# Converting float64 weights with bit operations on VectorE, and moving GpSimd's sums and low parts to VectorE

## The chip, the cores and the metric

The kernel runs on one core of a Trainium2 chip. Five engines work beside each other: TensorE (matmuls into PSUM), VectorE and ScalarE (elementwise work), GpSimd (elementwise work, on SBUF only) and SyncE, which here issues all DMAs. The metric is the device time of one execution in microseconds (us); less is better.

## The reference

Two stages of layers over q, k and v of shape (2, 6016, 256) in float32. The weights are float64 arrays.

```python
qn = q / (np.linalg.norm(q, axis=1, keepdims=True) + 1e-06)
kn = k / (np.linalg.norm(k, axis=1, keepdims=True) + 1e-06)
s = kn.transpose(0, 2, 1) @ qn / tau          # 256 x 256 for each batch
a = softmax(s)                                # rows, with 1e-9 in the divisor
x = (v @ a).reshape(12032, 256)
h = x @ w_in                                  # w_in 256 x 2048
x = (h - np.tanh(h)) @ w_out                  # w_out 2048 x 256
gate = 1 / (1 + np.exp(-(x @ w_gate)))        # w_gate, w_val 256 x 1536
out = (gate * (x @ w_val)) @ w_out2           # w_out2 1536 x 256
```

## The kernel before

**Tiling.** The tokens are cut into 24 blocks of 512 (12 for each batch). For a block, `emit_H` makes h for one of 16 column tiles of w_in, `emit_E` h - tanh(h) (two ScalarE squares L309 and L312, a tanh L310, a mask L313, and four VectorE instructions L314 to L317), `emit_gs` splits the result into two float32r parts (high: rounded by ScalarE, L322; low: the difference, L323), `emit_X` multiplies by w_out. `emit_GV` multiplies the block's result by one of 12 column tiles of w_gate and w_val, `emit_S` applies the sigmoid and the product (L387, L388), `emit_ps` splits it, `emit_O` multiplies by w_out2. Each of these products is made of three float32r matmuls of parts: high x high, low x high, high x low. v is split as a block (`split_v`), and so is the result of w_out (`emit_x2`). For block 0, and for the first two column tiles of its last product, the low parts are made by GpSimd, for all others by VectorE.

**The start.** Batch 0's q and k come in 19 chunks of mostly three tiles of 128 tokens, through six buffers (L498). TensorE adds up k^T q (`boot_s`, L507). ScalarE squares each chunk (L515) into one of two buffers, and the squares are added up in accb (L519): q's half by GpSimd, k's by VectorE, in the chunks 0 to 13; both by VectorE in 14 to 17. The last sums are joined (L521, L523), and `norm_mm` sums them over the partitions (L184). TensorE's queue has these matmuls ahead of the last chunk's products. The softmax (`s_softmax`) follows, and then a @ w_in, made once for each batch in chunks (`aw_chunk`), whose low part (L266) H needs.

**Weights.** `conv` brings a piece of float64 weights as pairs of 32-bit words. From the high word come sign, exponent and 20 bits of the mantissa: its absolute value (ScalarE, L121), a clamp (L124), mask and shift (L125), the sign (L128), all as bits of a float32. From the low word: ScalarE makes it a float (L122), VectorE takes the exponent of the first part (L131), GpSimd multiplies the two (L132); that is what the first part lacks. For w_in's eight pieces VectorE adds both (L135). For the 26 pieces of the other weights ScalarE rounds the first part to float32r (L137), and GpSimd makes the low part with a subtraction and an addition (L138, L139).

**Order.** The schedule is written by hand; every engine executes its instructions in the order of the program. A loop over steps T runs through the column tiles of all blocks: in a step stand H of tile T, E of tile T - 1, the split and X of tile T - 2, and pieces of the second layer of the block before. `conv` is a generator whose stages are spread over the steps through `at(step, ...)` and the list `running`: the DMA in one step, the first part in the next, the rounding and low parts in the one after. w_out's pieces are converted in the steps -1 to 13, w_in's last two in steps 6 and 8, those of the second layer from step 15 to 32, one for each step. Four of w_in's pieces are converted between the chunks of the start and two within the softmax. `e_mm` puts products of batch 1's first tokens into steps in which TensorE would wait. The tile pool cv has four buffers, of which a conversion takes two (bt and pt). Batch 1's squares are summed by GpSimd (L602), in the later blocks.

Of the kernel before, what the change touches and what calls it, by code (L numbers as in the profile page):

```python
# [8 lines left out]
F32 = mybir.dt.float32  # L9
F32R = mybir.dt.float32r  # L10
BF16 = mybir.dt.bfloat16
U32 = mybir.dt.uint32
# [5 lines left out]
P = 128  # L18
# h - tanh(h) = h^3 (C2 ((h^2 + CB)^2 + CG)) to 5e-7 for |h| <= HT; beyond HT the difference itself.
HT = 0.25  # L20
# [6 lines left out]
def kernel(  # L27
# [13 lines left out]
    nc = tc.nc  # L41
# [53 lines left out]
    def warm(n, name):  # L95
        """Matmuls that only keep the PE's clock up while it would wait."""
        o = psw(name, (P, P))
        for _ in range(n):
            MM(o, ones, ones, start=True, stop=True)

    aw_hi = [wp.tile([P, NK, 2 * P], F32R, name=f"awh{i}") for i in range(N1 // 2)]
    # until batch 0's a @ w_in is there, its low part's place holds w_in
    win = [wp.tile([P, NK, 2 * P], F32, tag=f"awl{i}", name=f"win{i}") for i in range(N1 // 2)]
# [5 lines left out]
    def conv(src, shape, pool, tag, name, w=None, hi=None, lo=None):  # L109
        """float64 words to float32 (w), or to its two float32r parts (hi, lo): three stages."""  # L110
        a, m = shape
        st = pool.tile([P, a, 2 * m], U32, tag=tag, name=f"st_{name}")
        nc.sync.dma_start(out=st, in_=src)
        yield
        words = st.rearrange("p a (m t) -> p a m t", t=2)
        low, high = words[:, :, :, 0], words[:, :, :, 1]
        bt = cv(f"cb_{name}", (P, a, m))
        pt = cv(f"cp_{name}", (P, a, m))
        bu, pu = bt.bitcast(U32), pt.bitcast(U32)
        lf = low.bitcast(F32)  # L120
        nc.scalar.activation(bt, high.bitcast(F32), AF.Abs)  # L121
        nc.scalar.activation(lf, low, AF.Copy, scale=2.0**-52)  # L122
        yield 1
        nc.vector.tensor_scalar(bt, bt, 2.0**-15, 122879.9921875, ALU.max, ALU.min)  # L124
        nc.vector.tensor_scalar(  # L125
            bu, bu, 0x07FFFFFF, 3, ALU.bitwise_and, ALU.logical_shift_left
        )
        nc.vector.scalar_tensor_tensor(  # L128
            out=bu, in0=high, scalar=0xC0000000, in1=bu, op0=ALU.bitwise_and, op1=ALU.bitwise_or
        )  # L130
        nc.vector.tensor_scalar(pu, bu, 0xFF800000, None, ALU.bitwise_and)  # L131
        nc.gpsimd.tensor_tensor(out=pt, in0=lf, in1=pt, op=ALU.mult)  # L132
        yield
        if w is not None:
            nc.vector.tensor_tensor(out=w, in0=bt, in1=pt, op=ALU.add)  # L135
        else:
            nc.scalar.activation(hi, bt, AF.Copy)  # L137
            nc.gpsimd.tensor_tensor(out=bt, in0=bt, in1=hi.bitcast(F32), op=ALU.subtract)  # L138
            nc.gpsimd.tensor_tensor(out=lo, in0=bt, in1=pt, op=ALU.add)  # L139

    def whole(g):
        """Only the stages of conv."""
        for x in g:
            if x is None:
                yield
# [14 lines left out]

# [1 line left out]
    kq = {}  # L162
# [5 lines left out]
    def s_mm(b, hi, lo, first, last):  # L168
        """hi, lo: [P, 2 (q, k), C] of one tile of tokens."""
        for ct in range(2):  # L170
            cs = slice(ct * P, (ct + 1) * P)
            o = kq[b][:, ct, :]
            MM(o, hi[:, 1, cs], hi[:, 0, :], start=first and ct == 0, stop=False, skip_group_check=True)
            MM(o, hi[:, 1, cs], lo[:, 0, :], start=False, stop=False, skip_group_check=True)
            MM(o, lo[:, 1, cs], hi[:, 0, :], start=False, stop=last, skip_group_check=True)
# [3 lines left out]
    def norm_mm(b, sq, sk, first, last):  # L179
        """Column sums of the tiles of sq (of q's squares) and sk (of k's), on c's partition."""  # L180
        for o, xs in ((0, sq), (2, sk)):
            for i, x in enumerate(xs):
                for ct in range(2):
                    MM(nrm[b][:, o + ct, :], x[:, ct * P:(ct + 1) * P], ones[:, :NW],  # L184
                       start=first and o + i + ct == 0, stop=last and i == len(xs) - 1, skip_group_check=True)

    def s_softmax(b, sq, sk):
        """sq, sk: tiles whose column sums are the sums of squares of q and k."""
        np_ = nrm.get(b)
# [9 lines left out]
        nc.vector.tensor_scalar(rn[:, 2:4], rn[:, 2:4], rtau[:, 0:1], None, ALU.mult)  # L199
        # q's factors as rows, the same on every partition: by the ones' product with their diagonal matrix  # L200
        dg = (cv if b else wk)(f"dg{b}", (P, 2, P))
# [51 lines left out]
    def aw_chunk(b, i, w):  # L253
        """Rows c of a @ w_in, columns of chunk i."""
        ap_ = psw(f"aw{b}_{i}", (P, 2, 2 * P))
        parts = [(aT[b], w)] if b == 0 else [(aT[b][0], w[0]), (aT[b][1], w[0]), (aT[b][0], w[1])]
        for n, (x, y) in enumerate(parts):
            for ct in range(2):
                for kk in range(2):
                    MM(ap_[:, ct, :], x[:, kk, ct * P:(ct + 1) * P], y[:, kk, :],  # L260
                       start=n + ct + kk == 0, stop=n == len(parts) - 1 and kk == 1, skip_group_check=True)
        yield
        if b == 0:
            aw_lo[i] = wp.tile([P, NK, 2 * P], F32R, tag=f"awl{i}", name=f"awl{i}")
        nc.scalar.activation(aw_hi[i], ap_, AF.Copy)
        nc.vector.tensor_tensor(out=aw_lo[i], in0=ap_, in1=aw_hi[i].bitcast(F32), op=ALU.subtract)  # L266

# [1 line left out]
    vn = {}  # L269
# [49 lines left out]

    def split(x, n, name, eng=None):  # L320
        hi, lo = rr(f"{name}h")[:, :n], rr(f"{name}l")[:, :n]
        nc.scalar.activation(hi, x, AF.Copy)  # L322
        (eng or nc.vector).tensor_tensor(out=lo, in0=x, in1=hi.bitcast(F32), op=ALU.subtract)  # L323
        return hi, lo

    def emit_gs(p, f):
        eng = nc.gpsimd if p == 0 else None
        ghl[p, f] = split(g_t.pop((p, f)), blocks[p][2], f"g{p}_{f}", eng)

# [18 lines left out]
    def emit_x2(p):  # L348
# [6 lines left out]
        else:  # L355
            # block 1's come before the last use of block 0's: these are where aT, acc and s1_split's are at other times
            h = [one_p.tile([P, TB], F32R, tag=t, name=f"x2{t}") for t in ("aT", "acc")]
# [33 lines left out]
    def emit_ps(p, m):  # L391
        phl[p, m] = split(p_t.pop((p, m)), blocks[p][2], f"p{p}_{m}", nc.gpsimd if p == 0 and m < 2 else None)

# [29 lines left out]

    # Batch 1's first J0 tiles of tokens, where the PE would wait: native float32 products of
    # what is loaded; their squares are summed later.
    JA, J0, GS = 20, 32, 5
# [37 lines left out]

# [1 line left out]
    rtau = const.tile([P, 1], F32, name="rtau")  # L466
# [12 lines left out]
    with tc.tile_pool(name="boot1", bufs=1) as boot1, tc.tile_pool(name="boot4", bufs=4) as boot4, \  # L479
# [30 lines left out]
        def boot_squares(i):  # L510
            """Squares, summed in accb; the last chunk's are left to the matmuls."""
            j, n = chunks[i]
# [3 lines left out]
            if i == NCH - 1:  # L516
                return [[sq[:, x, jj] for jj in range(n)] for x in range(2)]
            for x, e in enumerate((nc.gpsimd if i < NCH - 5 else nc.vector, nc.vector)):
                e.tensor_tensor(out=accb[:, x, :n], in0=accb[:, x, :n], in1=sq[:, x, :n], op=ALU.add)  # L519
            if i == F2:  # L520
# [7 lines left out]
        def load(i):  # L528
            """Chunk i of q and k, and what of w_in is converted along with it."""
            if i < NCH:  # L530
# [24 lines left out]
        while live:  # L555
            live = [g for g in live if next(g, live) is None]
        # the softmax's stages, and in between what does not wait for them: two of w_in's
        # conversions, v's first parts, batch 1's first products
        sm0 = s_softmax(0, *sq)
# [23 lines left out]

# [1 line left out]
    sraw = {}  # L585
# [44 lines left out]
    def s1_sum():  # L630
        """The sum over a group of tiles to that over all."""
        nc.vector.tensor_tensor(out=ks[1], in0=ks[1], in1=kq[1], op=ALU.add)

# [1 line left out]
    bg = {}  # L635
# [3 lines left out]

    # GV0: the steps of block 0's column tiles of w_gate and w_val; OFF..: those of the others', from  # L640
    # the first step of the block after
    GV0 = (20, 21, 22, 24, 25, 27, 28, 30, 31, 33, 34, 35)
# [140 lines left out]
```

## Time and profile before

| | us |
|---|---|
| median of 3 runs | 2437.92 (2436.18 to 2437.99) |
| the profiled execution: span | 2436.4 |
| TensorE (PE) busy | 2372.4 (97%) |
| VectorE (DVE) busy | 1841.3 (76%) |
| ScalarE (ACT) busy | 1606.9 (66%) |
| GpSimd (POOL) busy | 259.6 (11%) |

The profile gives the profiled execution's own time as its span, from the first instruction to the last; it lies within the three runs. In the rows, PE is TensorE's matmuls and PEld its weight loads. A float32 matmul (not float32r) appears as two instructions. "L314" is line 314 of the kernel. PEclk is the granted TensorE clock as a share of its full 2.4 GHz.

### The profile page before, as it was taken

The numbers are of one execution on the slowest core, as the hardware profiler recorded it, in microseconds if no ns is written. First come the engines' busy times: TensorE is split into PE (matmuls) and PEld (weight loads), VectorE is DVE, ScalarE is ACT, GpSimd is POOL, SyncE is SP. The second block draws the span as 40 slices with busy tenths as digits, with TensorE's granted clock in tenths as the row PEclk, the third lists the DMA queues.
The fourth block names the chain that finished last, engine by engine and source line by source line (L and its number), as shares of the span: only waits on it lengthen the run. The fifth ranks groups of instructions, "written<-read, shape, count | busy, mean of one in ns | idle before, by whom it ended". The sixth has DMA issues, their size and how long they took to land.

```text
span 2436.4 us, 29276 instructions
## 1 busy us (share of the span) xinstructions
PE 2372.4 (97%) x10408; PEld 1935.4 (79%) x10408; DVE 1841.3 (76%) x2791; ACT 1606.9 (66%) x2820; POOL 259.6 (11%) x171
## 2 busy tenths in 40 slices
PE   7868899999999999999999999999999999999999
PEld 6656678878888888788888888888888888888888
DVE  7899977778777777777777777777777777777764
ACT  4766666676766676776666766666666666666663
POOL 6466600111100000000000000000000000000000
PEclk9899999999999999999999999999999999999999
DMA  7432210111110110000100000000000000000000
GB/s 280 139 117 96 74 35 22 39 35 31 52 35 5 44 35 5 18 10 10 44 5 18 16 1 18 18 1 18 18 1 18 18 1 18 18 1 16 1 9 16
DMA packets 49106, 82.62 MB, mean 34 GB/s; under 512 B 4416, under 2 KB 18496, under 8 KB 48960
## 3 DMA queue, kind: packets, MB, share of 16 engines
q1 hardware_dynamic: 48960, 80.76, 10.0%
q8 instruction: 81, 1.33, 0.2%
q14 instruction: 65, 0.53, 0.1%
HBM read 65.80 MB, written 14.94 MB: 33 GB/s over the span
## 4 chain that ended last, share of the span: by engine, by line
PE 87%; DVE 7%; issue 3%; ACT 2%; POOL 1%; DMA 0%; SPq 0%; DVEq 0%; POOLq 0%; ACTq 0%
PE h L298 7%; PE x L344 7%; PE h L301 7%; PE h L299 7%; PE x L342 6%; PE x L341 6%; PE o L406 5%; PE o L405 5%; PE ga L377 5%; PE o L408 5%; PE ga L376 5%; PE va L377 5%; PE va L376 5%; PE va L379 5%; PE ga L379 5%
## 5 line engine op out<-in xcount | busy, mean ns | idle before, releaser
L314 DVE SCALAR_TENSOR_TENSOR w<-u,h 128x512 f32<-128x512 f32 (+1 forms) x384 | 259.1, 675 | 345.5 <-ACT t L310 345.1
L309 ACT ACTIVATE u<-h 128x512 f32<-128x512 f32 (+1 forms) x384 | 223.4, 582 | 256.7 <-PE h L301 256.4
L317 DVE COPY_PREDICATED w<-m,t 128x512 f32<-128x512 uint16 (+1 forms) x384 | 318.3, 829 | 41.0 <-DVE w L316 1.8
L298 PE MATMUL h<-vTh,awh 128*128 128x512 f32 (+1 forms) x768 | 303.8, 396 | 2.7 <-DVE t L315 1.9
L299 PE MATMUL h<-vTh,awl 128*128 128x512 f32 (+1 forms) x768 | 301.0, 392 | 4.2 <-DVE awl L266 4.2
L312 ACT ACTIVATE s<-u,cb 128x512 f32<-128x512 f32 (+1 forms) x384 | 274.0, 713 | 0.0
L313 ACT ACTIVATE m<-u,ct 128x512 bf16<-128x512 f32 (+1 forms) x384 | 272.3, 709 | 0.0
L316 DVE SCALAR_TENSOR_TENSOR w<-s,w 128x512 f32<-128x512 f32 (+1 forms) x384 | 264.3, 688 | 0.0
L315 DVE TENSOR_TENSOR t<-h,t 128x512 f32<-128x512 f32 (+1 forms) x384 | 258.0, 672 | 0.0
L301 PE MATMUL h<-vTl,awh 128*128 128x512 f32 (+1 forms) x768 | 237.6, 391 | 0.0
L310 ACT ACTIVATE t<-h 128x512 f32<-128x512 f32 (+1 forms) x384 | 223.7, 582 | 3.5 <-DVE w L314 0.8
L377 PE MATMUL va<-x2h,wvl 128*128 128x512 f32 (+1 forms) x552 | 216.2, 392 | 0.0
L377 PE MATMUL ga<-x2h,wgl 128*128 128x512 f32 (+1 forms) x552 | 216.1, 392 | 0.0
L376 PE MATMUL ga<-x2h,wgh 128*128 128x512 f32 (+1 forms) x552 | 215.9, 391 | 0.1
L376 PE MATMUL va<-x2h,wvh 128*128 128x512 f32 (+1 forms) x552 | 215.8, 391 | 0.0
L388 DVE TENSOR_TENSOR sg<-va,sg 128x512 f32<-128x512 f32 (+1 forms) x288 | 191.9, 666 | 19.7 <-PE va L379 18.8
L387 ACT ACTIVATE sg<-ga 128x512 f32<-128x512 f32 (+1 forms) x288 | 168.8, 586 | 16.6 <-PE ga L379 12.5
L379 PE MATMUL va<-x2l,wvh 128*128 128x512 f32 (+1 forms) x576 | 178.5, 391 | 0.0
L379 PE MATMUL ga<-x2l,wgh 128*128 128x512 f32 (+1 forms) x576 | 178.0, 390 | 0.0
L298 PEld LDWEIGHTS h<-vTh,awh 128*128 128x128 f32 x768 | 145.2, 189 | 36.6 <-DVE t L315 4.4
L299 PEld LDWEIGHTS h<-vTh,awl 128*128 128x128 f32 x768 | 144.9, 189 | 35.9 <-DVE awl L266 7.5
L301 PEld LDWEIGHTS h<-vTl,awh 128*128 128x128 f32 x768 | 144.2, 188 | 33.3
(396 smaller groups left out, 4772.0 us busy)
## 6 DMA issues: line engine op xcount, KB each, us to landing
v<-in_v_dram SPq DMA_DIRECT2D x22, 512.0 KB, 4.2
out_dram<-ob SPq DMA_DIRECT2D x22, 512.0 KB, 3.0
sr<-in_q_dram SPq DMA_DIRECT2D x47, 128.0 KB, 2.3
sr<-in_k_dram SPq DMA_DIRECT2D x47, 128.0 KB, 2.6
raw<-in_q_dram SPq DMA_DIRECT2D x13, 384.0 KB, 8.1
raw<-in_k_dram SPq DMA_DIRECT2D x13, 384.0 KB, 8.2
st_wi<-in_moe_w_in_dram SPq DMA_DIRECT2D x8, 512.0 KB, 7.3
er<-in_q_dram SPq DMA_DIRECT2D x16, 256.0 KB, 2.6
```

The lines of the kernel that those rows point to most:

```text
L298: MM(o[:, :n], aw_hi[i][:, kk, fs], h[:, kk, :n], start=kk == 0, stop=False)
L299: MM(o[:, :n], aw_lo[i][:, kk, fs], h[:, kk, :n], start=False, stop=False)
L301: MM(o[:, :n], aw_hi[i][:, kk, fs], lo[:, kk, :n], start=False, stop=kk == 1)
L312: nc.scalar.activation(s, u, AF.Square, bias=cb)
L313: nc.scalar.activation(m, u, AF.Relu, bias=ct2)
L314: nc.vector.scalar_tensor_tensor(out=w, in0=u, scalar=C2, in1=hp, op0=ALU.mult, op1=ALU.mult)
L315: nc.vector.tensor_tensor(out=t, in0=hp, in1=t, op=ALU.subtract)
L316: nc.vector.scalar_tensor_tensor(out=w, in0=s, scalar=CG, in1=w, op0=ALU.add, op1=ALU.mult)
L317: nc.vector.copy_predicated(w, m.bitcast(U16), t)
L376: MM(o[:, :n], wht[m // 2][:, d, ms], h[d][:, :n], start=d == 0, stop=False)
L377: MM(o[:, :n], wlt[m // 2][:, d, ms], h[d][:, :n], start=False, stop=False)
L379: MM(o[:, :n], wht[m // 2][:, d, ms], lo[d][:, :n], start=False, stop=d == 1)
```

## The change

The low word's bits 29 to 31 are put behind the first part's bits by one VectorE instruction, which makes the whole float32 (cut off, not rounded); what the float64 holds beyond that is left away. The low part is then the difference of this float32 and its rounding, made by VectorE. The squares of batch 0 are added in one VectorE instruction for q and k together, and all low parts of block 0 are VectorE's. Comments and docstrings are dropped too. The diff, without those and with lines left out:

```diff
         bt = cv(f"cb_{name}", (P, a, m))
-        pt = cv(f"cp_{name}", (P, a, m))
-        bu, pu = bt.bitcast(U32), pt.bitcast(U32)
-        lf = low.bitcast(F32)
+        bu = bt.bitcast(U32)
         nc.scalar.activation(bt, high.bitcast(F32), AF.Abs)
-        nc.scalar.activation(lf, low, AF.Copy, scale=2.0**-52)
         yield 1
...
-        nc.vector.tensor_scalar(pu, bu, 0xFF800000, None, ALU.bitwise_and)
-        nc.gpsimd.tensor_tensor(out=pt, in0=lf, in1=pt, op=ALU.mult)
-        yield
-        if w is not None:
-            nc.vector.tensor_tensor(out=w, in0=bt, in1=pt, op=ALU.add)
-        else:
+        nc.vector.scalar_tensor_tensor(
+            out=bu if w is None else w.bitcast(U32), in0=low, scalar=29, in1=bu,
+            op0=ALU.logical_shift_right, op1=ALU.bitwise_or
+        )
+        if w is None:
+            yield
             nc.scalar.activation(hi, bt, AF.Copy)
-            nc.gpsimd.tensor_tensor(out=bt, in0=bt, in1=hi.bitcast(F32), op=ALU.subtract)
-            nc.gpsimd.tensor_tensor(out=lo, in0=bt, in1=pt, op=ALU.add)
+            nc.vector.tensor_tensor(out=lo, in0=bt, in1=hi.bitcast(F32), op=ALU.subtract)
...
-    def split(x, n, name, eng=None):
+    def split(x, n, name):
...
-        (eng or nc.vector).tensor_tensor(out=lo, in0=x, in1=hi.bitcast(F32), op=ALU.subtract)
+        nc.vector.tensor_tensor(out=lo, in0=x, in1=hi.bitcast(F32), op=ALU.subtract)
...
-        eng = nc.gpsimd if p == 0 else None
-        ghl[p, f] = split(g_t.pop((p, f)), blocks[p][2], f"g{p}_{f}", eng)
+        ghl[p, f] = split(g_t.pop((p, f)), blocks[p][2], f"g{p}_{f}")
...
-        phl[p, m] = split(p_t.pop((p, m)), blocks[p][2], f"p{p}_{m}", nc.gpsimd if p == 0 and m < 2 else None)
+        phl[p, m] = split(p_t.pop((p, m)), blocks[p][2], f"p{p}_{m}")
...
-            for x, e in enumerate((nc.gpsimd if i < NCH - 5 else nc.vector, nc.vector)):
-                e.tensor_tensor(out=accb[:, x, :n], in0=accb[:, x, :n], in1=sq[:, x, :n], op=ALU.add)
+            nc.vector.tensor_tensor(out=accb[:, :, :n], in0=accb[:, :, :n], in1=sq[:, :, :n], op=ALU.add)
```

## Rows read from the trace of the kernel before

**Rows 1.** Busy time of each engine (instructions) by stretch, granted clock, DMA share

```profile
core 0: us, PE busy (x) PEld busy (x) DVE busy (x) ACT busy (x) POOL busy (x), PEclk, DMA share, GB/s
0.00:48.40 48.40, 45.91 (x194) 39.14 (x194) 34.28 (x33) 24.30 (x23) 31.88 (x22) 1.00 0.81 294
48.40:62.77 14.37, 0.00 (x2) 0.03 (x1) 12.80 (x16) 6.32 (x7) 5.77 (x3) 0.65 0.58 197
62.77:83.89 21.12, 18.28 (x71) 15.06 (x72) 12.13 (x29) 11.26 (x23) 2.58 (x2) 0.76 0.44 145
83.89:176.74 92.85, 74.41 (x299) 56.08 (x297) 88.49 (x116) 66.09 (x118) 64.05 (x43) 0.96 0.38 123
176.74:301.71 124.97, 105.39 (x406) 77.25 (x407) 121.31 (x163) 86.27 (x153) 81.34 (x51) 0.95 0.28 91
...
700.00:800.00 100.00, 100.00 (x431) 80.77 (x430) 76.08 (x116) 68.75 (x121) 7.41 (x5) 1.00 0.08 25
```

**Rows 2.** Timeline of PE from 3 to 63 us: start, duration, what, idle before

```profile
7.03 41.37 PE L507 MATMUL kq<-raw 128*128 128x256 f32 x180 [0.62 <-DMA raw<-in_k_dram]
62.77 0.45 PE L184 MATMUL n<-ones,accb 128*128 128x64 f32 x1 [14.37 <-DVE accb L523]
```

**Rows 3.** DVE's instructions by form, 0 to 62 us: busy us, mean ns, idle

```profile
L519 DVE TENSOR_TENSOR accb<-accb,sq 128x768 f32<-128x768 f32 x14 | 24.0, 1722 | 2.9 <-ACT sq L515 2.6
L135 DVE TENSOR_TENSOR win<-cb_wi,cp_wi 128x512 f32<-128x512 f32 x4 | 9.1, 2280 | 4.7 <-POOL cp_wi L132 4.7
```

**Rows 4.** Waits, 0 to 62 us: total us, times, longest

```profile
ACT sq L515 <- POOL accb L519: 15.9, 4, 4.2
```

**Rows 5.** DVE's instructions by form, 85 to 310 us

```profile
L317 DVE COPY_PREDICATED w<-m,t 128x512 f32<-128x512 uint16 x33 | 51.2, 1550 | 3.8 <-DVE w L316 0.5
L316 DVE SCALAR_TENSOR_TENSOR w<-s,w 128x512 f32<-128x512 f32 x33 | 29.0, 879 | 0.0
...
L323 DVE TENSOR_TENSOR p_2l<-sg,p_2h 128x512 fp32r<-128x512 f32 x1 | 1.8, 1809 | 0.0
```

**Rows 6.** The same, 1300 to 2300 us

```profile
L317 DVE COPY_PREDICATED w<-m,t 128x512 f32<-128x512 uint16 x170 | 126.7, 745 | 17.9 <-DVE w L316 0.5
...
L316 DVE SCALAR_TENSOR_TENSOR w<-s,w 128x512 f32<-128x512 f32 x170 | 115.7, 681 | 0.0
...
L286 DVE TENSOR_TENSOR vTl<-v,vTh 128x1024 fp32r<-128x1024 f32 x10 | 12.3, 1226 | 14.8 <-ACT vTh L284 14.8
```

**Rows 7.** Timeline of DVE, 250.9 to 257 us: one step of the full stage

```profile
250.93 0.42 DVE L124 TENSOR_SCALAR cb_m<-cb_m 128x512 f32<-128x512 f32 x1
251.38 0.43 DVE L125 TENSOR_SCALAR cb_m<-cb_m 128x512 uint32<-128x512 uint32 x1
251.85 0.69 DVE L128 SCALAR_TENSOR_TENSOR cb_m<-st_m,cb_m 128x512 uint32<-128x512 uint32 x1
252.57 0.43 DVE L131 TENSOR_SCALAR cp_m<-cb_m 128x512 uint32<-128x512 uint32 x1
252.92 0.68 DVE L323 TENSOR_TENSOR g_9l<-w,g_9h 128x512 fp32r<-128x512 f32 x1
253.52 0.68 DVE L314 SCALAR_TENSOR_TENSOR w<-u,h 128x512 f32<-128x512 f32 x1
254.12 0.68 DVE L315 TENSOR_TENSOR t<-h,t 128x512 f32<-128x512 f32 x1
254.72 0.68 DVE L316 SCALAR_TENSOR_TENSOR w<-s,w 128x512 f32<-128x512 f32 x1
255.50 1.67 DVE L317 COPY_PREDICATED w<-m,t 128x512 f32<-128x512 uint16 x1
```

**Rows 8.** Timeline of DVE around 1512 us

```profile
1512.46 0.74 DVE L317 COPY_PREDICATED w<-m,t 128x512 f32<-128x512 uint16 x1
1513.09 0.68 DVE L388 TENSOR_TENSOR sg<-va,sg 128x512 f32<-128x512 f32 x1
```

**Rows 9.** Timeline of DVE in the softmax

```profile
77.97 1.29 DVE L135 TENSOR_TENSOR win<-cb_wi,cp_wi 128x512 f32<-128x512 f32 x2 [1.46 <-POOL cp_wi L132]
79.18 0.69 DVE L266 TENSOR_TENSOR awl<-aw,awh 128x512 fp32r<-128x512 f32 x1
```

**Rows 10.** Waits, 310 us to the end: total us, times, longest

```profile
DVE g_9l L323 <- ACT g_9h L322: 15.4, 19, 1.8
```

## The prediction

> **What bounds the kernel now.** I cut the run at the points where the kind of work changes and asked for each engine's busy time there [rows 1]. Before 48.40 us TensorE multiplies batch 0's k and q, nearly without a gap; from 48.40 to 62.77 it does nothing and its granted clock falls to 0.65; then comes the softmax, with the clock at 0.76; from 83.89 to 301.71 it is VectorE that is full, 88.49 of 92.85 us and 121.31 of 124.97 us, or 95% and 97%; and from then on TensorE is busy all the time (700 to 800 us stands for the rest: 431 instructions in 100 us, 0.232 us each). The change touches nothing after about 317 us, so of 2436.4 us only the first eighth can move.
>
> Second, the start in detail. TensorE's products run unbroken from 7.03 us for 41.37 us, and what follows waits 14.37 us for VectorE's last sum of squares [rows 2]. That sum is late because VectorE and GpSimd share it and get in each other's way: an addition of 768 columns takes VectorE 1.72 us on the mean, and the addition that completes w_in 2.28 us for 512 [rows 3]; the squares on ScalarE then wait 15.9 us for buffers that GpSimd has not yet read [rows 4].
>
> Third, what VectorE's time between 85 and 310 us consists of. The masked copy (L317) takes 1.55 us, the product before it (L316) 0.88, a low part of p 1.81 [rows 5]. In a stretch where GpSimd is nearly idle the same copy takes 0.745 us and the product 0.681 [rows 6]; a low part of 512 columns not held up takes 0.68 [rows 7]. So VectorE is full, but partly with waiting inside its own instructions. From these means the 33 copies and 33 products hold 33 x (0.805 + 0.198) = 33 us of it, seven low parts of p like the one shown 7 x 1.13 = 8 us, and some first steps of conversions more. GpSimd is busy 145 us in those stages [rows 1].
>
> **Part by part.** I cost VectorE by the distance between the starts of following instructions, since their records overlap by some 0.08 us. From one step [rows 7]: the conversion's clamp 0.45, mask and shift 0.47, sign 0.72 (the next one needs its result), a low part 0.60, L314 and L315 0.60 each, L316 0.78; L317 takes 0.63 when not held up [rows 8]. One E step is thus 2.61 us.
>
> *Conversion.* Removed: L122 on ScalarE, L131 on VectorE, the product on GpSimd, and its two low-part instructions (or VectorE's L135 for w_in). Added on VectorE: one shift-and-or, and for 26 of the 34 weight pieces one subtraction. No trace shows the shift-and-or. Its nearest row is L128, the same instruction form on the same strided words, 0.69 us [rows 7]; half of that is the lower bound (the rate of L125 beside it), twice it the upper. I take L128's, 0.60 to the next start, because operands and form are equal. A conversion then costs 0.45 + 0.47 + 0.72 + 0.60 = 2.24 us, with a subtraction 2.84.
>
> *Start.* GpSimd's halves of 14 sums come to VectorE. An addition of 1536 columns is not in the trace; 1024 columns take 1.22 us [rows 6] and 512 take 0.68, so about 1.77. Thirteen of them are 23.0 us, the two small first chunks 1.9, four conversions 9.0, and the last three chunks and the two joins 3.7: 37.6 us, less than the 41.4 us in which TensorE makes its products, while ScalarE is busy only 24.3 us of the first 48.4 [rows 1]. Six chunk buffers lie between the loads and the consumers, and the loads, on SP's queue, already keep TensorE fed; with squares done earlier their slots come free no later. Hence the norm's matmuls start when TensorE gets to them, at 48.4 instead of 62.77: 14.4 us less at best, which I shorten to 14.0. If VectorE loses 10% on hand-overs it ends near 51: 11 is the other end.
>
> *Softmax.* With TensorE no longer idle its clock should not drop. The 71 instructions there would be 71 x 0.232 = 16.5 us instead of 18.28: up to 1.8, on the path only in part, as some lie beside the softmax on VectorE. GpSimd's product no longer stands between L131 and win: VectorE waits 1.46 us for it and then has two additions to do ahead of awl, which is what H waits for [rows 9]; 0.8 us. One ScalarE instruction fewer lies ahead of the first E. I take 2.5, ends 0.8 and 3.5. No DMA is added, removed or moved on SP's queue; the stores of win wait less. One cv buffer of four per conversion instead of two can only free transfers earlier.
>
> *VectorE's stage, first part (E 0 to 15).* 16 E steps 41.8, 16 low parts of g, GpSimd's until now, 9.6, seven of aw 4.2, conversions of w1 (7 x 2.24 + 8 x 0.60) 20.5, two of w_in 4.5, one of the second pair 2.2, v's low part 1.1: 84 us where 92.85 are taken. *Second part (E 16 to 31).* 41.8 + 9.6, nine low parts of p 5.4, nine products with the sigmoid 5.4, 16 conversions 45.4, x2's and v's low parts 2.3: 110 us for 124.97. TensorE's floor is below both: 299 x 0.232 = 69 and 406 x 0.232 = 94 us. Filled as now (96%), VectorE needs 194 / 0.96 = 202 us for these 217.8: 16 us less. With no gaps at all it is 24; with TensorE taking over in steps where 18 matmuls for gate, value and output come on top, it is less, down to 8.
>
> *New waits.* The subtraction stands behind ScalarE's rounding of the same weights, and on VectorE the next piece's bit operations, the low part of g and E are queued behind it. In the late stage a low part that waits for such a rounding loses 15.4 / 19 = 0.8 us [rows 10]; nothing is the lower bound. 25 such waits would be 20 us. I take nearly nothing: ScalarE issues the rounding straight behind the sigmoid, while VectorE still has the masked copy and the product to do. The low parts of block 0 wait for ScalarE likewise, but now, as VectorE is full, it meets them late. Removing GpSimd's waits costs nothing elsewhere: what stays there are batch 1's squares, unchanged.
>
> Sum: 14.0 + 2.5 + 16 = 32.5 us. The profiled span, 2436.4 us, is 1.5 below the median of 2437.92; 2437.92 - 32.5 gives **2405 us**.
>
> **Rivals.** *A, the full stage gives nothing back.* The new waits cost their 0.8 us 20 times over, or TensorE is the next limit at once. For it: 97% leaves no room, and a gate-and-value step has 30 matmuls, 7.0 us, against 7.2 of VectorE. Against: over the whole second part TensorE needs 94 us where VectorE needs 110. Only start and softmax remain: 2437.9 - 16.5 = 2421 us. Chance 0.17.
>
> *B, the shift-and-or costs twice L128.* 27 more times 0.69 us in the full stage, 19 us; in the start the four still nearly fit. 2424 us; the bits of L125 and L128 already run at the rates of their forms, which speaks against. Chance 0.04. The same if the loads hold up the start: half of the 14 us, 2412. Chance 0.06.
>
> *C, slower: VectorE is simply full and the moved work adds to it.* The stretched durations would then be VectorE's own here, from its inputs, and not GpSimd's doing. In the stage it gains 18 low parts x 0.68, 27 shift-and-ors x 0.69 and 25 subtractions x 0.68, 48 us, and loses 27 x 0.43 + 2 x 0.68, 13 us: 35 us more, with the start no earlier: 2473 us. It decides as soon as L317 stays above 1.2 us with GpSimd idle. Against it: the same form takes 0.745 late [rows 6]. Chance 0.04. The Trainium skill, Perfetto Trace Analysis, Optimizing Scalar/DVE Operations, speaks for this side: if VectorE is saturated, it says, moving some of its work to ScalarE or even GpSimd may make sense, and this change does the reverse. By that rule alone the time would be C's. The same paragraph adds that the two share an SBUF port, so that shifting work between them may not help; the trace bears out this half, with 1.55 against 0.745 us for one instruction.
>
> **The numbers.** Forecast 0.65, of which most between 2396 and 2414 by the ends above; A 0.17, B and the loads 0.10, C 0.04; 0.04 for more than the forecast's best end. The range 2394 to 2420 leaves out that, C, B and half of A, under 0.2. A measurement of this kernel tells 0.2%, about 5 us, from no change; all cases but C lie further down, and I leave 0.03 for mishaps that cancel. Faster 0.93, same 0.03, slower 0.04.
>
> **What would show it.** The norm's first matmul between 48 and 51 us with no drop of the clock ahead of it; L317 at 0.75 us and L316 at 0.68 from the first step on; GpSimd with nothing to do between 3 us and batch 1's squares, which begin beyond 400 us; the step of E 32 some 32 us before 301.71; VectorE still above 90% until then. Wrong if L317 stays long, if VectorE waits for ScalarE at the conversions' subtractions, if TensorE is full from block 1's first gate step on, or if the shift-and-or is not near 0.69 us.

## The result and the profile after

The changed kernel takes 2396.11 us (median of 4 runs, 2395.97 to 2396.57) where the kernel before takes 2437.95 (4 runs beside it): 41.8 us less, a ratio of 0.9828 with a 95% interval of 0.9814 to 0.9842. The forecast was 2405 us with a range of 2394 to 2420: the direction and the places hold, the size was 9 us too small. The profiled span is 2394.9 us.

The same stretches as in [rows 1], cut at the same events (first matmul of the norm, E 0, E 16, E 32), in the changed kernel; columns as there. E n is the start of VectorE's first instruction in the step E of column tile n, counted through the blocks.

```profile
0.00:47.86 47.86, 45.46 (x194) 38.66 (x195) 37.35 (x40) 28.39 (x25) 2.02 (x7) 1.00 0.96 350
47.86:65.41 17.55, 13.27 (x68) 10.80 (x69) 11.62 (x26) 9.83 (x21) 0.00 (x0) 1.00 0.59 197
65.41:149.39 83.98, 73.88 (x302) 57.70 (x300) 81.29 (x137) 60.84 (x108) 0.00 (x0) 0.96 0.43 135
149.39:260.83 111.44, 100.09 (x404) 79.01 (x405) 107.01 (x183) 76.30 (x135) 0.00 (x0) 0.94 0.33 102
...
700.00:800.00 100.00, 100.00 (x431) 80.79 (x431) 76.29 (x115) 68.59 (x120) 8.92 (x6) 1.00 0.08 25
```

The gap of 14.37 us has gone as a stage: what took 62.77 us up to the norm takes 47.86. The softmax stage falls from 21.12 to 17.55 us at a full clock, the two parts of VectorE's stage from 92.85 to 83.98 and from 124.97 to 111.44. That is 14.9 + 3.6 + 8.9 + 13.5 = 40.9 us; the last 0.7 comes in the steps just behind, and from about 290 us on the two kernels stay the same distance apart. VectorE is 97% and 96% busy in its stage, just as before: the share does not show what happened there. Summed instruction by instruction against the mean of the same form in the changed kernel, VectorE's records between E 0 and E 32 were 52 us too long before; the work added to it, less what was taken off, is 34 us by the same means. Most of the 22 us that the stage lost is the difference of the two.

TensorE's timeline at the start, which answers to [rows 2] (start, duration, what, idle before):

```profile
6.75 40.91 PE L503 MATMUL kq<-raw 128*128 128x256 f32 x180 [0.45 <-DMA raw<-in_k_dram]
47.86 1.10 PE L181 MATMUL n<-ones,accb 128*128 128x64 f32 x8 [0.20 <-DVE accb L518]
```

VectorE's groups by form, the first from 0 to 48 us, the others from 68 to 280 us, which answer to [rows 3, 5] (busy us, mean ns, idle before):

```profile
L514 DVE TENSOR_TENSOR accb<-accb,sq 128x1536 f32<-128x1536 f32 x13 | 22.8, 1754 | 2.9 <-ACT sq L511 2.1
...
L314 DVE COPY_PREDICATED w<-m,t 128x512 f32<-128x512 uint16 x35 | 26.0, 742 | 4.0 <-DVE w L313 0.5
...
L313 DVE SCALAR_TENSOR_TENSOR w<-s,w 128x512 f32<-128x512 f32 x34 | 23.2, 683 | 0.0
...
L129 DVE SCALAR_TENSOR_TENSOR cb_m<-st_m,cb_m 128x512 uint32<-128x512 uint32 x18 | 12.5, 693 | 0.6
...
L136 DVE TENSOR_TENSOR w1l<-cb_w,w1h 128x512 fp32r<-128x512 f32 x8 | 5.5, 682 | 0.0
```

The masked copy has fallen from 1550 to 742 ns, the product before it from 879 to 683. One sum of 1536 columns takes 1754 ns; VectorE's half alone took 1722 before, and GpSimd's beside it 2132 (kernel before, 0 to 62 us):

```profile
L519 POOL TENSOR_TENSOR accb<-accb,sq 128x768 f32<-128x768 f32 x12 | 25.6, 2132 | 2.1 <-ACT sq L515 1.6
```

The new shift-and-or (L129) takes 693 ns, L128's time in the kernel before. The new subtractions (L136) wait for nothing: 0.0 us of idle time before them.

### The profile page after: what moved, and what is told of

Read it like the earlier page. It is cut to its first block, busy times and chain, and to the rows that moved or that the text cites. A ratio compares the mean times of both kernels' runs of the same rounds, so it can differ in the third digit from the quotient of the medians.

```text
span 2394.9 us, 29032 instructions
## 1 busy us (share of the span) xinstructions
PE 2361.2 (99%) x10408; PEld 1934.4 (81%) x10408; DVE 1808.3 (76%) x2823; ACT 1588.2 (66%) x2786; POOL 67.7 (3%) x53
## 4 chain that ended last, share of the span: by engine, by line
PE 89%; DVE 7%; ACT 2%; issue 1%; DMA 0%; SPq 0%; DVEq 0%; ACTq 0%
PE h L295 7%; PE h L296 7%; PE h L298 7%; PE x L340 7%; PE x L337 7%; PE x L338 7%; PE o L402 5%; PE ga L373 5%; PE o L401 5%; PE va L372 5%; PE ga L372 5%; PE va L373 5%; PE va L375 5%; PE o L404 5%; PE ga L375 5%
## 5 line engine op out<-in xcount | busy, mean ns | idle before, releaser
L314 DVE COPY_PREDICATED w<-m,t 128x512 f32<-128x512 uint16 (+1 forms) x384 | 290.5, 757 | 40.7 <-DVE w L313 1.4
L313 DVE SCALAR_TENSOR_TENSOR w<-s,w 128x512 f32<-128x512 f32 (+1 forms) x384 | 257.6, 671 | 0.0
```

What stands on the lines that cost most here:

```text
L313: nc.vector.scalar_tensor_tensor(out=w, in0=s, scalar=CG, in1=w, op0=ALU.add, op1=ALU.mult)
L314: nc.vector.copy_predicated(w, m.bitcast(U16), t)
```

## The experiments

Three runs undo one part each, two put GpSimd back without giving it anything useful to do, three take instructions from VectorE, two look at the clock. Differences in us are between medians, against the changed kernel's 2396.11; ratios are against the kernel before, as measured beside each run. Line numbers in the rows are those of each run's own kernel.

**Squares back on GpSimd.**

```diff
-            nc.vector.tensor_tensor(out=accb[:, :, :n], in0=accb[:, :, :n], in1=sq[:, :, :n], op=ALU.add)
+            for x, e in enumerate((nc.gpsimd if i < NCH - 5 else nc.vector, nc.vector)):
+                e.tensor_tensor(out=accb[:, x, :n], in0=accb[:, x, :n], in1=sq[:, x, :n], op=ALU.add)
```

> The changed kernel, but q's squares of chunks 0 to 13 are added by GpSimd again. Theory (GpSimd and VectorE hold each other up, start limited by their sum): the norm's first matmul goes back from 47.9 us to 58 to 61 us, TensorE idles 10 to 13 us ahead of it, its clock falls there and the softmax stage takes 19 to 21 us instead of 17.6; after that nothing changes; 2407 to 2412 us. Rival (the start was long because of GpSimd's product within the conversions of w_in, not because of the squares): norm below 53 us, time below 2402.

Measured: 2410.93 us, 14.8 more; ratio 0.9888 (0.9873 to 0.9903). The two stretches ahead of and behind the norm's first matmul, in this run, columns as above:

```profile
48.00:58.60 10.60, 0.10 (x1) 0.03 (x1) 9.54 (x14) 5.13 (x6) 0.63 (x1) 0.68 0.56 209
58.60:80.48 21.88, 18.28 (x71) 15.04 (x72) 11.71 (x26) 10.38 (x22) 0.00 (x0) 0.76 0.44 144
```

TensorE waits again, the granted clock falls to 0.68 and then 0.76 of its full 2.4 GHz (so for a good part of the time it is at the lower level, 1.2 GHz), and the softmax stage takes 21.88 us instead of 17.55. The rest is unchanged within 0.6 us: E 16 starts 15.06 us later than in the changed kernel, E 0 15.07, E 50 14.5. The theory holds. VectorE's halves take 955 ns there, not the 1722 of before; what is held up here are the conversions between them (0 to 58 us):

```profile
L515 DVE TENSOR_TENSOR accb<-accb,sq 128x768 f32<-128x768 f32 x14 | 13.3, 955 | 4.7 <-ACT sq L511 4.3
L126 DVE SCALAR_TENSOR_TENSOR cb_wi<-st_wi,cb_wi 128x512 uint32<-128x512 uint32 x4 | 8.9, 2222 | 0.1
L122 DVE TENSOR_SCALAR cb_wi<-cb_wi 128x512 f32<-128x512 f32 x4 | 8.2, 2043 | 0.0
```

The clamp L122 takes 2043 ns where it needs some 420, and it has one input: not only instructions with two inputs are held up.

**Block 0's low parts back on GpSimd.**

```diff
...
-        ghl[p, f] = split(g_t.pop((p, f)), blocks[p][2], f"g{p}_{f}")
+        ghl[p, f] = split(g_t.pop((p, f)), blocks[p][2], f"g{p}_{f}", nc.gpsimd if p == 0 else None)
...
-        phl[p, m] = split(p_t.pop((p, m)), blocks[p][2], f"p{p}_{m}")
+        phl[p, m] = split(p_t.pop((p, m)), blocks[p][2], f"p{p}_{m}", nc.gpsimd if p == 0 and m < 2 else None)
```

> The changed kernel, but GpSimd makes block 0's low parts of g and the first two of p again. Theory (each of GpSimd's reads costs VectorE about as much as the instruction it takes off): first part of the full stage between 4 us shorter and 8 us longer, total 2394 to 2404 us. Rival (VectorE's count of instructions alone decides, GpSimd beside it is free): 18 x 0.60 = 11 us less, down to what TensorE allows, 2385 to 2390.

Measured: 2398.68 us, 2.6 more; ratio 0.9838 (0.9823 to 0.9852). From E 0 to E 32 it takes 195.78 us, the changed kernel 195.42: VectorE has 18 instructions fewer and gains nothing. In the first part of the stage (68 to 153 us) the shift-and-or is what waits:

```profile
L129 DVE SCALAR_TENSOR_TENSOR cb_w<-st_w,cb_w 128x512 uint32<-128x512 uint32 x8 | 11.3, 1419 | 0.3
...
L126 DVE SCALAR_TENSOR_TENSOR cb_w<-st_w,cb_w 128x512 uint32<-128x512 uint32 x7 | 5.9, 849 | 0.2
...
L122 DVE TENSOR_SCALAR cb_wi<-cb_wi 128x512 f32<-128x512 f32 x2 | 3.0, 1522 | 0.0
```

In these three groups 8 x 0.73 + 7 x 0.16 + 2 x 1.10 = 9 us are given back, out of 18 x 0.60 = 11 saved; summed over all of VectorE's records from E 0 to E 32, against the means of the changed kernel, it is 11.6 us, all of it. So the rival falls, and moving this part was worth next to nothing by itself. The 2.6 us of difference lie ahead of E 0, which in the profiled execution starts 2.62 us later: 1 us up to the norm and 1.65 us in a softmax stage at a granted clock of 0.91. This edit does not reach there; why the clock was lower in that execution stays open.

**The old conversion.** The function `conv` as it was, everything else changed:

```diff
-        nc.vector.scalar_tensor_tensor(
-            out=bu if w is None else w.bitcast(U32), in0=low, scalar=29, in1=bu,
-            op0=ALU.logical_shift_right, op1=ALU.bitwise_or
-        )
+        nc.vector.tensor_scalar(pu, bu, 0xFF800000, None, ALU.bitwise_and)
+        nc.gpsimd.tensor_tensor(out=pt, in0=lf, in1=pt, op=ALU.mult)
+        yield
...
-            nc.vector.tensor_tensor(out=lo, in0=bt, in1=hi.bitcast(F32), op=ALU.subtract)
+            nc.gpsimd.tensor_tensor(out=bt, in0=bt, in1=hi.bitcast(F32), op=ALU.subtract)
+            nc.gpsimd.tensor_tensor(out=lo, in0=bt, in1=pt, op=ALU.add)
```

> The changed kernel with the old conversion (ScalarE's second pass, GpSimd's product, subtraction and addition). Theory: GpSimd's 78 instructions of 1.3 to 1.7 us hold up VectorE's two-input instructions in the full stage: L317's form back at 1.3 us or more on the mean, the stage 15 to 25 us longer although VectorE has about 24 us of instructions fewer; start and softmax 0 to 4 us longer; 2412 to 2425 us. Rival (what mattered were squares and low parts): under 2405.

Measured: 2426.69 us, 30.6 more; ratio 0.9952 (0.9935 to 0.9968). From E 0 to E 32 it takes 215.87 us, 20.5 more, as expected; start and softmax cost 9.8, more than I had written, so the total lies past my bound. VectorE's timeline between the squares, and GpSimd's beside it, show most of why, a wait for GpSimd's product at every conversion of w_in:

```profile
24.62 1.75 DVE L517 TENSOR_TENSOR accb<-accb,sq 128x1536 f32<-128x1536 f32 x1
27.57 0.69 DVE L135 TENSOR_TENSOR win<-cb_wi,cp_wi 128x512 f32<-128x512 f32 x1 [1.19 <-POOL cp_wi L132]
28.17 3.62 DVE L517 TENSOR_TENSOR accb<-accb,sq 128x1536 f32<-128x1536 f32 x2
```

```profile
24.84 2.69 POOL L132 TENSOR_TENSOR cp_wi<-st_wi,cp_wi 128x512 f32<-128x512 f32 x1 [6.38 <-DVE cp_wi L131]
```

GpSimd's product, started at 24.84 us beside VectorE's sum, takes 2.69 us there, and L135 then waits 1.19 us for it, four times in all (4.8 us). The norm starts at 54.34 us, 6.5 later, and behind TensorE's idle 5.12 us ahead of it the clock is lower here too (0.77 in a softmax stage of 20.91 us). In the full stage the masked copy is at 1401 ns on the mean of 31. This run also brings back ScalarE's second pass and the second buffer of a conversion, and does not tell them apart from GpSimd's reads; the next one adds reads alone.

**GpSimd reads, for nobody.** After each of the 26 conversions:

```diff
+        if w is None:
+            for _ in range(3):
+                nc.gpsimd.tensor_tensor(out=low.bitcast(F32), in0=bt, in1=bt, op=ALU.mult)
```

> The changed kernel; after each conversion of the 26 split pieces GpSimd also multiplies the result by itself three times, into the staging tile, which nobody reads: 78 instructions of GpSimd and no new work for any other engine. Theory (hold-up inside VectorE's instructions): masked copy at 1.2 us or more on the mean in the full stage, 20 to 35 us longer, 2416 to 2431 us. Rival (the old kernel lost its time by waiting for GpSimd's results): less than 4 us longer, under 2400.

Measured: 2431.57 us, 35.5 more; ratio 0.9975 (0.9964 to 0.9985). E 0 starts 0.22 us later, E 34 35.87 us later: everything is lost in the full stage, and no engine reads what GpSimd makes. From E 0 to E 32 the stage is 33.4 us longer, and VectorE's records, against the means of the changed kernel, are too long by 33.4 us in sum: the loss lies inside them. The total lies 0.6 us past my bound; on the masked copy I was wrong, it is at 1031 ns on the mean (30 of them), and the product ahead of it at 1224: which instruction is held up depends on where GpSimd's reads fall. One step of VectorE's timeline, then GpSimd's:

```profile
233.26 0.69 DVE L129 SCALAR_TENSOR_TENSOR cb_m<-st_m,cb_m 128x512 uint32<-128x512 uint32 x1
233.87 0.68 DVE L323 TENSOR_TENSOR g_8l<-w,g_8h 128x512 fp32r<-128x512 f32 x1
234.47 1.53 DVE L323 TENSOR_TENSOR p_4l<-sg,p_4h 128x512 fp32r<-128x512 f32 x1
235.92 0.67 DVE L314 SCALAR_TENSOR_TENSOR w<-u,h 128x512 f32<-128x512 f32 x1
236.52 0.68 DVE L315 TENSOR_TENSOR t<-h,t 128x512 f32<-128x512 f32 x1
237.12 1.44 DVE L316 SCALAR_TENSOR_TENSOR w<-s,w 128x512 f32<-128x512 f32 x1
238.66 0.74 DVE L317 COPY_PREDICATED w<-m,t 128x512 f32<-128x512 uint16 x1
```

```profile
234.08 3.93 POOL L135 TENSOR_TENSOR st_m<-cb_m 128x512 f32<-128x512 f32 x3 [4.94 <-ACT m L313]
```

Three products fill 234.08 to 238.01. The low part of p, with both inputs in SBUF, takes 1.53 us; L314 and L315, which read h from PSUM, take their usual 0.67 and 0.68; L316, again with both inputs in SBUF, takes 1.44. The page "SBUF — State Buffer" of the Trainium skill, section "Who interferes with whom", says so: a VectorE instruction with two SBUF inputs contends with a GpSimd instruction that reads SBUF, and the contention is an exclusive lock. The run agrees: 1.44 and 1.53 us instead of 0.68, and 0.67 and 0.68 for the two with PSUM.

**GpSimd writes only.** Instead of the three products, four fills of the used staging tile:

```diff
+        if w is None:
+            for _ in range(4):
+                nc.gpsimd.memset(st, 0)
```

> The changed kernel; after each conversion of the 26 split pieces GpSimd also fills the used staging tile (1024 columns) with zeros four times: it writes and reads nothing. Theory A (only GpSimd's reads hold up VectorE's two-input instructions): masked copy stays at 0.75 us, at most the clamp and the mask-and-shift get longer, 0 to 8 us more, 2396 to 2404 us. Theory B (any access of GpSimd to SBUF does): as with three products, 10 us more or above, 2406 us or above.

Measured: 2396.58 us, 0.5 more, within the runs' spread; ratio 0.9835 (0.9819 to 0.9852). GpSimd does 104 such fills, 99 us of work, as much as the 78 products of the run before (98.9 us), on the same staging tiles, and VectorE's copy keeps its time. VectorE's copy, GpSimd's fills, and GpSimd's products of the run before:

```profile
L317 DVE COPY_PREDICATED w<-m,t 128x512 f32<-128x512 uint16 x35 | 26.1, 746 | 4.0 <-DVE w L316 0.5
```

```profile
L135 POOL MEMSET st_m<- 128x1024 uint32 x72 | 68.7, 954 | 59.2 <-ACT m L313 26.8 <-ACT t L310 16.8 <-ACT s L312 9.8
L135 POOL MEMSET st_w<- 128x1024 uint32 x32 | 30.5, 954 | 109.8 <-DVE cb_w L129 74.2 <-ACT m L313 17.8 <-ACT awh L265 16.4
```

```profile
L135 POOL TENSOR_TENSOR st_m<-cb_m 128x512 f32<-128x512 f32 x54 | 68.7, 1272 | 85.3 <-ACT m L313 69.9 <-ACT t L310 12.6
L135 POOL TENSOR_TENSOR st_w<-cb_w 128x512 f32<-128x512 f32 x24 | 30.2, 1258 | 119.4 <-DVE cb_w L129 84.0 <-ACT awh L265 19.4 <-ACT m L313 14.7
```

It is GpSimd's reading, not its activity, that costs these VectorE instructions time. The fills fall beside E and the low parts. Of the stage's 27 clamps, which have one input, one alone started beside a fill, and it took 0.64 us where the form takes 0.42; so for such instructions the fills are not shown to be free:

```profile
152.99 0.64 DVE L122 TENSOR_SCALAR cb_m<-cb_m 128x512 f32<-128x512 f32 x1
```

```profile
150.38 2.97 POOL L135 MEMSET st_m<- 128x1024 uint32 x3
```

**Without the shift-and-or,** for the 26 split pieces:

```diff
-        nc.vector.scalar_tensor_tensor(
-            out=bu if w is None else w.bitcast(U32), in0=low, scalar=29, in1=bu,
-            op0=ALU.logical_shift_right, op1=ALU.bitwise_or
-        )
+        if w is not None:
+            nc.vector.scalar_tensor_tensor(
+                out=w.bitcast(U32), in0=low, scalar=29, in1=bu, op0=ALU.logical_shift_right, op1=ALU.bitwise_or
+            )
```

> The changed kernel without the shift-and-or for the 26 split pieces: their last three bits of the mantissa are left out. Theory (VectorE alone sets the pace of the full stage, by the sum of the distances of its starts): 25 x 0.60 = 15 us less of VectorE's work in the stage, of which 10 to 15 come off the time, 2381 to 2386 us. Rival (TensorE or ScalarE is the next limit already): less than 5 us, 2391 or above. In either case the distance to the changed kernel is the price of that one instruction in place.

Measured: 2381.08 us, 15.0 less; ratio 0.9768 (0.9753 to 0.9782). The full 25 x 0.60 us come off.

**Without absolute value and clamp:**

```diff
-        nc.scalar.activation(bt, high.bitcast(F32), AF.Abs)
         yield 1
...
-        nc.vector.tensor_scalar(bt, bt, 2.0**-15, 122879.9921875, ALU.max, ALU.min)
         nc.vector.tensor_scalar(
-            bu, bu, 0x07FFFFFF, 3, ALU.bitwise_and, ALU.logical_shift_left
+            bu, high, 0x07FFFFFF, 3, ALU.bitwise_and, ALU.logical_shift_left
         )
```

> The changed kernel without ScalarE's absolute value and VectorE's clamp: mask and shift read the high word itself. It leaves out the guard for weights outside float32's range; inside it the bits are the same. VectorE has 25 x 0.45 = 11 us less in the full stage, if mask and shift from every second word cost what they cost now (0.43 us), and 5 us less if they take 0.69. Theory (VectorE sets the pace): 2384 to 2391 us. Rival (another engine is the limit already): 2393 or above.

Measured: 2383.21 us, 12.9 less; ratio 0.9777 (0.9762 to 0.9792). It is a little beyond my lower bound: mask and shift from every second word cost no more, and all 27 clamps (27 x 0.45 = 12.2) come off:

```profile
L121 DVE TENSOR_SCALAR cb_m<-st_m 128x512 uint32<-128x512 uint32 x18 | 7.6, 422 | 0.0
```

For weights inside float32's range this version makes, by its code, the same bits in less time than either kernel. Its price is the guard: a weight outside that range would come out wrong instead of being clamped.

**Both of these removals.**

```diff
-        nc.scalar.activation(bt, high.bitcast(F32), AF.Abs)
...
-        nc.vector.tensor_scalar(bt, bt, 2.0**-15, 122879.9921875, ALU.max, ALU.min)
...
+        if w is not None:
+            nc.vector.scalar_tensor_tensor(
+                out=w.bitcast(U32), in0=low, scalar=29, in1=bu, op0=ALU.logical_shift_right, op1=ALU.bitwise_or
+            )
```

> The changed kernel without absolute value and clamp, and without the shift-and-or for the 26 split pieces (three bits of the mantissa left out). VectorE loses 25 x 1.05 = 26 us of the full stage. The single removals brought 15 and 13 us. If VectorE still sets the pace, 28 us: 2367 to 2370 us. If TensorE takes over on the way (its instructions alone fill some 165 of the stage's 196 us), 18 to 25 us: 2371 to 2378 us. That is what I expect.

Measured: 2375.97 us, 20.1 less, where the two alone brought 15.0 + 12.9 = 27.9; ratio 0.9746 (0.973 to 0.9763). The two parts of the stage in this run:

```profile
64.32:138.72 74.40, 69.88 (x305) 56.64 (x303) 71.71 (x118) 55.40 (x98) 0.00 (x0) 1.00 0.48 154
138.72:239.11 100.39, 96.07 (x409) 77.43 (x408) 90.01 (x149) 68.59 (x121) 0.00 (x0) 0.98 0.35 114
```

The first part is 9.6 us shorter than in the changed kernel, a little more than the two removals brought there one by one (4.9 + 3.6); the second is 11.1 us shorter, where they brought 9.8 + 8.6. There VectorE is down to 90% and TensorE up to 96%. TensorE's 714 instructions at 0.232 us are 166 us of the 175 that are left: here, as it seems, rival A's limit comes in, some 20 us further down than the change got.

**The clock behind an idle TensorE.** The kernel with the squares on GpSimd, with matmuls nobody reads in the gap:

```diff
+                warm(20, "warm1")
                 nrm[0] = psw("n0", (P, 4, NW))
```

> The changed kernel with q's squares of chunks 0 to 13 back on GpSimd, and 20 float32 matmuls of 128 columns on TensorE, about 10 us, that nobody reads, in the time in which it waits for the sums. Theory (the softmax stage is longer behind an idle TensorE because its clock is lower): granted clock at 0.95 or more, the softmax stage 17.5 to 18.5 us instead of 21.9 without them; 3 to 5 us less than without them, 2406 to 2408 us. Rival (the stage is longer for another reason, such as the order of loads): 20 us or more, 2409 to 2412 us.

Measured: 2410.7 us, ratio 0.9889 (0.9874 to 0.9904): no difference to the run without them. The time is in the rival's range, but the matmuls filled only 4.63 us, less than half of the gap; TensorE then stood still for 6.47 us, the clock was 0.77 in the next stage, and that stage took 21.47 us, about as long as without them:

```profile
48.34 4.63 PE L99 MATMUL warm<-ones 128*128 128x128 f32 x40
59.45 1.94 PE L181 MATMUL n<-ones,accb 128*128 128x64 f32 x8 [6.47 <-DVE accb L519]
```

```profile
59.45:80.92 21.47, 19.19 (x76) 15.82 (x77) 11.71 (x26) 10.37 (x22) 0.00 (x0) 0.77 0.44 146
```

This does not tell the two theories apart, so a run with 48 matmuls followed:

> As the run with 20 matmuls in the gap, which filled only 4.6 of 11 us and left the clock falling, but with 48, about 11.1 us. Theory (clock): granted clock in the softmax stage 0.95 or more, its first 20 matmul records at half the time (n 1.0 us instead of 1.9), the stage 17.5 to 18.5 us instead of 21.9; 2406 to 2408 us. Rival (another reason): stage 20 us or more at a full clock, 2409 to 2412 us.

Measured: 2408.00 us, 2.9 less than with the gap; ratio 0.9877 (0.986 to 0.9893). The intervals of the two ratios overlap, so the time by itself settles little; the trace does. TensorE's timeline:

```profile
48.76 10.88 PE L99 MATMUL warm<-ones 128*128 128x128 f32 x96
59.47 1.00 PE L181 MATMUL n<-ones,accb 128*128 128x64 f32 x8
60.31 1.08 PE L503 MATMUL kq<-raw 128*128 128x256 f32 x4
```

The granted clock is 1.00 before and behind, the norm's first 8 records take 1.00 us where they took 1.94, and E 0 starts 17.9 us behind the norm instead of 21.9.

## Why the prediction was right, and where its size was off

**The start: right.** 14.0 us were taken, with 14.4 as the best end; 14.9 were measured. VectorE's 37.6 us of work, as summed from 1224 and 680 ns rows, came to 37.35 us busy, and the norm is released by VectorE 0.20 us after TensorE is through: the two end together. With VectorE at the end of its work too, there was no room left for a longer sum. The additional 0.5 us is a start of TensorE's products 0.28 us earlier and a product chain that ran 0.46 us shorter; it means little, since in four runs with the same start (block 0's low parts, GpSimd's reads, its fills, no shift-and-or) the norm begins between 48.38 and 48.83 us, 13.9 to 14.4 earlier than before. The run with the squares alone undone puts the wait back.

**The softmax: right in kind, the term too small.** 2.5 us taken, 3.5 as the upper end, 3.6 measured. I had counted the clock as "up to 1.8, on the path only in part" and GpSimd's product as 0.8. The 1.8 itself was too small: it took for each of the 71 instructions the 0.232 us of the late matmuls, which are of another shape. At a full clock TensorE is busy 13.27 us there, 5 us less than the 18.28 of before. The runs show the clock as the larger part by far: with GpSimd's squares back and no product of GpSimd's in the way, the stage is at 21.88 us, as long as before; with matmuls in the gap it is at 17.9. It is on the path nearly in full, as the norm's and the last k^T q matmuls stand in a row there: 5.4 us before ([rows 2] is their beginning), 2.9 after.

**VectorE's stage: the term that was mis-sized.** The sums of distances between starts, 84 and 110 us, met 83.98 and 111.44, and not by luck: the 16 E steps of the first part, 41.8 us in the sum, take 41.8 in the trace, the 16 low parts of g 9.6 for 9.6, the ten sign instructions of its conversions 0.73 us each for 0.72. The step that failed is the one behind them: "Filled as now (96%), VectorE needs 194 / 0.96 = 202 us". I took the 4% outside VectorE's busy time as time lost and divided by what is left. But those 4% are for the most part breaks between an instruction and the next one that needs its result, and the distances had them in them already; one step after the change, to be compared with [rows 7]:

```profile
236.30 0.69 DVE L126 SCALAR_TENSOR_TENSOR cb_m<-st_m,cb_m 128x512 uint32<-128x512 uint32 x1
237.03 0.69 DVE L129 SCALAR_TENSOR_TENSOR cb_m<-st_m,cb_m 128x512 uint32<-128x512 uint32 x1
237.64 0.68 DVE L320 TENSOR_TENSOR g_12l<-w,g_12h 128x512 fp32r<-128x512 f32 x1
238.24 0.68 DVE L311 SCALAR_TENSOR_TENSOR w<-u,h 128x512 f32<-128x512 f32 x1
238.84 0.69 DVE L312 TENSOR_TENSOR t<-h,t 128x512 f32<-128x512 f32 x1
239.44 0.68 DVE L313 SCALAR_TENSOR_TENSOR w<-s,w 128x512 f32<-128x512 f32 x1
240.22 0.75 DVE L314 COPY_PREDICATED w<-m,t 128x512 f32<-128x512 uint16 x1
```

0.73, 0.61, 0.60, 0.60, 0.60, 0.78: the distances of before, with the short breaks behind L126 and L313 in them and the usual overlaps elsewhere. Without the division the term is 217.8 - 194 = 23.8; 22.4 was measured, and the whole forecast would have been 14.0 + 2.5 + 23.8 = 40.3 against 41.8.

**New waits: right.** Nothing was taken for the subtraction behind ScalarE's rounding, and nothing is lost there.

**The rivals.** A, that the full stage gives nothing back, fell: of TensorE's two floors the nearer one, 94 us, is still below 111, and only with another 26 us off VectorE does TensorE get in the way. B fell: the shift-and-or takes 693 ns; the loads did not hold up the start, where TensorE's products run unbroken, though the DMAs' share there rose from 0.81 to 0.96. C fell clearly: VectorE executes 48 us of added instructions in that stage and gets through it 22 us sooner. The rule behind C, to relieve a full VectorE, was tried by giving 18 low parts back to GpSimd: the 11 us saved came back as hold-ups, 9 of them in the three groups shown. Of the paragraph of the Trainium skill that the prediction names there (Perfetto Trace Analysis, Optimizing Scalar/DVE Operations), this run bears out the second half, that shifting work between the two may not help.

**How the parts add up.** Undone one by one they cost 14.8, 2.6 and 30.6 us, 48 together, for a change of 41.8. They are not independent: with the old conversion the start is late already and the clock is lost, so putting the squares and the low parts back as well costs less (41.8 - 30.6 = 11.2 us).

## What to carry to other kernels

Where VectorE is full and GpSimd reads SBUF beside it, look at the durations of its instructions beside the same forms in a stretch where GpSimd rests: here 0.8 us per masked copy was time spent waiting for GpSimd's reads, and it counted as busy. Work handed from VectorE to GpSimd is then not work saved: 18 low parts brought nothing, and 78 reads that nobody needed cost 35 us. Sum up VectorE's time by the distances between the starts of following instructions, and do not divide that sum by a busy share again.

## What the runs showed of the hardware that was not expected

GpSimd's fills, 104 of 954 ns beside the same VectorE instructions, cost 0.5 us or nothing, while 78 products of 1.27 us cost 35.5: equal busy time of GpSimd, and no common price for it. Behind 4.63 us of matmuls and a gap of 6.47 us in TensorE's work its granted clock was 0.77 in the next stage, the same as with the old conversion behind a gap of 5.12 us without such matmuls. And a clamp with a single input was held up by GpSimd's additions like the instructions with two: 2043 ns for some 420.
